# State matmuls of a block attention kernel: two halves of 64 columns in place of one of 128

## The chip, the cores and the metric

The kernel runs on one core of one Trainium2 chip. Its engines are TensorE (matmuls; in the profile PE, and PEld for its weight loads), VectorE (DVE), ScalarE (ACT), GpSimd (POOL) and SyncE (SP), which here issues loads, stores and transposing transfers. The metric is the device time of one execution in microseconds; less is better. A time of the kernel is the median of several executions. A profile is one execution, taken by the hardware's profiler.

## The reference

Two stages follow each other. The first is attention with a decaying state, per batch (4) and head (8), over 768 positions in blocks of 64, with 64 values a head:

```
intra = (qb @ kb.T) * Dmask          # within the block
intra = intra @ vb
inter = (qb * lam_pow) @ kv_state    # what earlier blocks left
out   = intra + inter
kv_state = lam_block * kv_state + (kb * rev_pow).T @ vb
```

The second takes the output as 3072 tokens of 512 values and computes `h = x @ w_in` (2048 wide), `g = h + sin(alpha*h)**2 / alpha`, and `g @ w_out`. Inputs and output are float32; the kernel's matmuls run in bfloat16 and sum in float32.

## The kernel before

The kernel cuts each batch's sequence into six blocks of 128 positions, 24 blocks in all (s = 0 to 23). The decay is multiplied into queries and keys ahead of time (lines 464 and 471), so the state is a plain running sum in a bank of TensorE's accumulation memory, which starts anew with each batch. Two heads share the 128 partitions, so each block has four pairs of heads (`jp`).

What one block needs of TensorE is put into one operation of the planner, `piece_G`, with these parts, issued one after the other by `run`:

- `inter` (line 603): the state times the queries. For each of the four pairs of heads one matmul with the tile `Zd`, 128 by 128, which holds the two heads' 64 by 64 states on its diagonal and zeros elsewhere. The moving operand is 128 columns of `qkT`, taken as two runs of 64.
- `part_S` (line 543) of the next block: keys times queries, eight matmuls, each with 64 rows of the array (64*128).
- `part_O` (line 623): the masked scores `Sm` times the values, eight matmuls, each with 64 columns of the array (128*64); they add to what `inter` left in the same bank.
- `part_Z` (line 568): keys times values, eight matmuls (128*64), added to the state.

`inter` with `Zd` is used from block 13 on, where `wide` is true: for blocks 13 to 17 and 19 to 23 (blocks 12 and 18 begin a batch and have no earlier state). That makes ten groups. In nine of them a `part_S` follows `inter`; the last, of block 23, has none, and `part_O` follows directly. Blocks 1 to 5 and 7 to 11 use another form, line 616: a compact state `Zc` and eight matmuls on 64 rows and 64 columns (64*64).

After the group, VectorE multiplies the scores by the mask (line 552), ScalarE or VectorE copies the block's output into `xT` (line 632), and the state into `Zd` (line 578). The wide layer is done in units: `unit_A` (line 671, four matmuls of 512 columns from `xT`), followed by a sine and a square on ScalarE or GpSimd and a sum on VectorE, and `unit_B` (line 736, four matmuls into the output's bank). `unit_A2` (line 705) is a variant with 256 columns. From block 12 on, units A and B alternate, with one attention group after every three to five pairs of them.

A planner (`_Plan`) sets the order on each engine before the kernel is built: it simulates all operations with durations written by hand and dependences found from the buffers that each reads and writes, and emits one wait for each dependence that the order on one engine does not cover. A group counts there as 0.55 us for `part_O` with `inter` (0.68 in the form with `Zc`), 0.33 for `part_S`, 0.13 for `part_Z` and 0.1 for the whole. A group is one operation: it waits ahead of its first matmul and signals after its last.

Of the kernel before, what the change touches and what calls it, by code (L numbers as in the profile page):

```python
# [32 lines left out]
class _Plan:  # L33
# [20 lines left out]
    def op(self, eng, emit, dur, reads=(), writes=(), dma=None, after=(), issue=0.4, lat=2.6, runs=64):  # L54
        o = _Op(eng, emit, dur, tuple(reads), tuple(writes), dma, after, issue, lat, runs)
        for b in o.reads:
            if b in self.writer:
                o.deps.add(self.writer[b])
        for b in o.writes:
            if b in self.writer:  # L60
                o.deps.add(self.writer[b])
            o.deps.update(self.readers.get(b, ()))
        o.deps.update(after)
        for b in o.reads:
            self.readers.setdefault(b, []).append(o)
        for b in o.writes:
            self.writer[b] = o
            self.readers[b] = []
        o.deps.discard(o)
        o.lead = self.lead  # L70
        self.ops.append(o)
        return o
# [171 lines left out]
def bass_lightning_attn__then__act_snake_kernel(  # L244
# [35 lines left out]
    with es:  # L280

        def sb(name, shape, dt):
            return es.enter_context(nc.sbuf_tensor(name, shape, dt))

        def ring(name, n, shape, dt):
            return [sb(f"{name}_{i}", shape, dt) for i in range(n)]
# [17 lines left out]
        qkT = sb("qkT", [128, RT, 8, 128], BF16)  # L304
        Sm = ring("Sm", 2, [128, 8, 128], BF16)
        Zc = ring("Zc", 2, [128, 4, D], BF16)
        Zd = ring("Zd", 2, [128, 4, 128], BF16)
# [17 lines left out]
        ps = [banks[:, 512 * i:512 * i + 512] for i in range(8)]  # L325
# [4 lines left out]
        def _(_unused_eng):  # L330
# [7 lines left out]
            def bank(i):  # L338
                return ("bank", i)
# [249 lines left out]
            def part_O(s, ob, ob2=None):  # L589
                n, j, jq, u = s % NB, s % R2, s % RT // 2 * 2, slice(64 * (s % 2), 64 * (s % 2) + 64)  # L590
                c, i4 = s // BPC, s % BPC
                obs = [ob, ob] if ob2 is None else [ob, ob2]
                new = (0,) if ob2 is None else (0, 2)
                reads = [("v2", j), ("qT", jq), ("qT", jq + 1), ("Sm", s % 2)]
                wide = n and s > SD
                if wide:
                    reads += [("Zd", (s - 1) % 2, 0), ("Zd", (s - 1) % 2, 1)]
                elif n:
                    reads += [("Zc", (s - 1) % 2)]

                def inter(e):
                    for jp in range(4):
                        ins = e.matmul(  # L603
                            ps[obs[jp // 2]][:, 128 * jp:128 * (jp + 1)].rearrange("p (t x) -> p t x", x=64),
                            Zd[(s - 1) % 2][:, jp, :], qkT[:, jq:jq + 2, jp, u],
                            start=(jp in new), stop=False, skip_group_check=True,
                        )
                    return ins

                def mm(e):  # L610
                    ins = None
                    if n and not wide:
                        for jp in range(4):
                            for h in range(2):
                                r = slice(64 * h, 64 * h + 64)
                                e.matmul(
                                    ps[obs[jp // 2]][r, 128 * jp:128 * (jp + 1)].rearrange("p (t x) -> p t x", x=64),
                                    Zc[(s - 1) % 2][r, jp, :], qkT[r, jq:jq + 2, jp, u],
                                    start=(jp in new), stop=False, skip_group_check=True,
                                )  # L620
                    for jp in range(4):
                        for h in range(2):
                            ins = e.matmul(  # L623
                                ps[obs[jp // 2]][64 * h:64 * h + 64, 128 * jp:128 * (jp + 1)],
                                v2[j][:, 2 * jp + h, :], Sm[s % 2][:, 4 * h + jp, :],
                                start=(n == 0 and jp in new), stop=(jp == 3), skip_group_check=True,
                            )
                    return ins

                def then():  # L630
                  for eng, a0, a1, dur in ((("ACT", 0, 2, 0.45), ("DVE", 2, 4, 0.4)) if ob2 is not None else (((("ACT", 0.73, 0.4), ("DVE", 0.7, 0.0)), 0, 4, 0),)):
                    op(eng, lambda e, a0=a0, a1=a1: (e.copy if e is nc.scalar else e.tensor_copy)(  # L632
                        xT[c % RX][:, a0:a1, BL * i4:BL * (i4 + 1)].rearrange("p a (x t) -> p a t x", t=2),
                        ps[obs[a0 // 2]][:, 128 * a0:128 * a1].rearrange("p (a t x) -> p a t x", t=2, x=64)), dur,
                       [bank(obs[a0 // 2])], [("xT", c % RX, i4, a) for a in range(a0, a1)])

                return mm, (0.55 if wide else 0.68) if n else 0.35, reads, [bank(b) for b in sorted(set(obs))], then, inter if wide else None
# [194 lines left out]
            for i in range(NM):  # L832
                hb = (6, 0, 3, 1, 2, 5)[i % 6] if i < 10 else (3, 0, 1, 2)[i % 4]
                u = unit_A2(0, i // 2 * 2, i % 2, hb) if i < 2 else unit_A(0, i, hb)
# [23 lines left out]
            for i in range(8):  # L858
                unit_A2(1, 2 * i, 1, (5, 6, 4)[(i + 2) % 3])
                for _ in range(2 if i in (0, 4) else 1):  # L860
                    kind, s = pieces.pop(0)
# [68 lines left out]
```

## Time and profile before

| | us |
|---|---|
| median of 3 runs | 223.14 (222.13 to 223.4) |
| profiled execution, its own time | 223.52 |
| its span, first to last instruction | 221.4 |
| TensorE busy | 208.6 |
| ScalarE busy | 155.9 |
| VectorE busy | 122.6 |
| GpSimd busy | 89.1 |

The span is shorter than the execution's own time, which also has what lies around the program's instructions. Line 603 has 40 matmuls in the profile, the first at 98.9 us and the last group at 172.2 us.

A line of a group of instructions or of the timeline names the kernel's line (L603), the operation, the tiles as output<-inputs, the part of the array in use as rows*columns, the shape of the moving operand, and how many instructions there are (x4). Matmuls are pipelined: the end of one is modelled and lies behind the start of the next, so distances are taken from start to start.

### The profile page before, as it was taken

How to read it: one execution, taken by the hardware profiler on the slowest of the kernel's cores; microseconds unless marked ns; L12 is line 12 of the kernel's file. 1: busy time of each engine (PE TensorE's matmuls, PEld its weight loads, DVE VectorE, ACT ScalarE, POOL GpSimd, SP SyncE). 2: the span in 40 equal slices, each digit the busy share in tenths (PEclk: the TensorE clock that was granted, in tenths of full speed). 3: DMA queues.
4: the chain of work that ended last, by engine and by line, in shares of the span. 5: the costliest groups of instructions: out<-in, count | busy, mean ns of one | idle time of the engine just before them, and what ended most of it. 6: DMA issues, size and time to landing. Idle time of an engine off the chain costs nothing.

```text
span 221.4 us, 4062 instructions
## 1 busy us (share of the span) xinstructions
PE 208.6 (94%) x1645; PEld 110.7 (50%) x1645; DVE 122.6 (55%) x184; ACT 155.9 (70%) x277; POOL 89.1 (40%) x100
## 2 busy tenths in 40 slices
PE   3889987899898999999999999999999999999995
PEld 1446433456575785545445444545545444444444
DVE  4687775354777887667655455645465544445100
ACT  3735994347697997788788887877788677778211
POOL 4386763454978776863576103011001011110100
DMA  5999999999999999999999752110110011101112
GB/s 131 236 232 271 206 214 208 217 235 237 233 245 275 242 191 245 219 254 189 276 240 245 155 112 33 47 50 0 47 50 21 26 47 50 47 0 49 75 70 95
DMA packets 83651, 33.31 MB, mean 150 GB/s; under 512 B 63520, under 2 KB 80688, under 8 KB 83632
## 3 DMA queue, kind: packets, MB, share of 16 engines
q1 hardware_dynamic: 76880, 24.25, 53.6%
q0 software_dynamic: 3696, 3.67, 9.9%
q10 hardware_dynamic: 3056, 5.13, 6.4%
q8 instruction: 13, 0.21, 0.4%
q14 instruction: 6, 0.05, 0.1%
HBM read 27.28 MB, written 6.29 MB: 152 GB/s over the span
## 4 chain that ended last, share of the span: by engine, by line
PE 63%; DMA 24%; POOL 4%; SPq 4%; ACT 2%; DVE 1%; issue 1%
PE bank L736 32%; PE bank L671 24%; DMA k<-in_k_dram 10%; DMA q<-in_q_dram 5%; DMA v<-in_v_dram 4%; DMA w<-in_moe_w_in_dram 4%; SPq L342 4%; PE bank L705 3%; PE bank L623 2%; PE bank L543 2%; POOL qk L471 1%; POOL qk L464 1%; PE bank L603 1%; POOL u L720 1%; DVE gT L723 1%
## 5 line engine op out<-in xcount | busy, mean ns | idle before, releaser
L736 PE MATMUL bank<-w,gT 128*128 128x512 bf16 (+1 forms) x400 | 94.8, 371 | 0.0
L688 DVE SCALAR_TENSOR_TENSOR gT<-u,rinv,bank 128x512 bf16<-128x512 bf16 x74 | 54.6, 746 | 51.7 <-ACT u L685 34.2
L671 PE MATMUL bank<-xT,w 128*128 128x512 bf16 x296 | 74.2, 379 | 0.6 <-DVE gT L688 0.6
L681 ACT ACTIVATE t<-bank,alpha 128x512 bf16<-128x512 f32 x74 | 50.6, 686 | 24.1 <-PE bank L671 24.0
L736 PEld LDWEIGHTS bank<-w,gT 128*128 128x128 bf16 x400 | 37.7, 98 | 39.6
L686 POOL TENSOR_TENSOR u<-t 128x512 bf16<-128x512 bf16 x19 | 19.7, 1040 | 80.7 <-ACT t L681 79.7
L671 PEld LDWEIGHTS bank<-xT,w 128*128 128x128 bf16 x296 | 28.5, 98 | 34.9 <-DVE gT L688 1.1
L685 ACT ACTIVATE u<-t 128x512 bf16<-128x512 bf16 x55 | 34.4, 629 | 1.8 <-DVE gT L723 0.3
L552 DVE TENSOR_TENSOR Sm<-bank,mask 128x1024 bf16<-128x1024 f32 x24 | 29.2, 1222 | 10.3 <-PE bank L568 7.7
L464 POOL TENSOR_TENSOR qk<-q,Lq 128x512 bf16<-128x512 f32 x24 | 24.5, 1044 | 21.7 <-DMA q<-in_q_dram 18.1
L471 POOL TENSOR_TENSOR qk<-k,Lk 128x512 bf16<-128x512 f32 x22 | 22.9, 1044 | 7.2 <-DMA k<-in_k_dram 7.0
L749 ACT COPY osb<-bank 128x512 f32<-128x512 f32 (+1 forms) x25 | 14.2, 569 | 14.8 <-PE bank L736 14.8
L705 PE MATMUL bank<-xT,w 128*128 128x256 bf16 x176 | 22.3, 273 | 2.0 <-DVE gT L723 2.0
L723 DVE SCALAR_TENSOR_TENSOR gT<-u,rinv,bank 128x256 bf16<-128x256 bf16 x44 | 19.1, 476 | 7.2 <-POOL u L720 4.1
L715 ACT ACTIVATE t<-bank,alpha 128x256 bf16<-128x256 f32 x44 | 18.5, 471 | 3.3 <-PE bank L705 3.1
L705 PEld LDWEIGHTS bank<-xT,w 128*128 128x128 bf16 x176 | 16.2, 98 | 5.5 <-DVE gT L723 3.0
L473 ACT CAST v<-v 128x512 bf16<-128x512 f32 x18 | 11.0, 615 | 7.6 <-DMA v<-in_v_dram 7.6
L632 ACT CAST xT<-bank 128x512 bf16<-128x512 f32 (+1 forms) x18 | 12.9, 716 | 2.8 <-PE bank L568 1.6
L720 POOL TENSOR_TENSOR u<-t 128x512 bf16<-128x512 bf16 x11 | 11.3, 1039 | 4.7 <-ACT t L715 4.6
L543 PE MATMUL bank<-qkT 64*128 64x128 bf16 x192 | 9.8, 226 | 0.2 <-DVE qkT L493 0.2
L623 PE MATMUL bank<-Sm,v 128*64 128x128 bf16 x192 | 9.9, 225 | 0.0
L829 PE MATMUL bank<-mask,ident 128*128 128x512 bf16 x12 | 5.7, 564 | 3.7 <-DVE mask L429 3.7
(55 smaller groups left out, 111.4 us busy)
## 6 DMA issues: line engine op xcount, KB each, us to landing
k<-in_k_dram SPq DMA_DIRECT2D x24, 256.0 KB, 5.5
v<-in_v_dram SPq DMA_DIRECT2D x24, 256.0 KB, 5.5
q<-in_q_dram SPq DMA_DIRECT2D x10, 512.0 KB, 5.5
out_dram<-osb ACTq DMA_DIRECT2D x19, 256.0 KB, 2.0
w<-in_moe_w_out_dram POOLq DMA_DIRECT2D x4, 512.0 KB, 13.1
w<-in_moe_w_in_dram POOLq DMA_DIRECT2D x3, 512.0 KB, 9.0
q<-in_q_dram SPq DMA_DIRECT2D x4, 256.0 KB, 4.6
ws<-in_moe_w_in_dram SPq DMA_DIRECT2D x2, 512.0 KB, 5.4
```

The lines of the kernel that those rows point to most:

```text
L464: lambda e, a=a: e.tensor_tensor(qk2[:, j:j + 2, 4 * a:4 * a + 4, :], q32[jq][:, 4 * a:4 * a + 4, :, :].rearrange("p h t d -> p t h d"), b ...
L471: lambda e: e.tensor_tensor(qk2[:, j, H:2 * H, :], k32[jl][:, :, :], lk, ALU.mult), 0.7 if s in (0,1) else 1.05,
L552: op("DVE", lambda e: e.tensor_tensor(Sm[s % 2][:, :, :], banks[:, 512 * b0:512 * b0 + 1024].rearrange("p (c i) -> p c i", i=128), mask[:, ...
L671: ins = e.matmul(ps[hb][:, c0:c1], w1[:, kc, 128 * m:128 * (m + 1)], xT[x][:, kc, c0:c1], start=(kc == 0 and c0 == lo), stop=(kc == NKC - ...
L681: op("ACT", lambda e: e.activation(t16[ju][:, w], ps[hb][:, w], ACTF.Sin, scale=alpha[:, m:m + 1]), 0.69 * f, [bank(hb), "alpha"], [("t16" ...
L685: lambda e: (e.activation(u16[ju][:, w], t16[ju][:, w], ACTF.Square) if e is nc.scalar else e.tensor_tensor(u16[ju][:, w], t16[ju][:, w], ...
L686: e.tensor_tensor(u16[ju][:, w], t16[ju][:, w], t16[ju][:, w], ALU.mult)), 0,
L688: op("DVE", lambda e: e.scalar_tensor_tensor(out=gT[g][:, m, w], in0=u16[ju][:, w], scalar=rinv[:, m:m + 1], in1=ps[hb][:, w], op0=ALU.mul ...
L705: ins = e.matmul(ps[hb][:, 256 * i:256 * i + 256], w1[:, kc, 128 * (m + i):128 * (m + i + 1)], xT[x][:, kc, lo:lo + 256], start=(kc == 0 a ...
L715: op("ACT", lambda e, i=i: e.activation(t16[ju][:, 256 * i:256 * i + 256], ps[hb][:, 256 * i:256 * i + 256], ACTF.Sin, scale=alpha[:, m + ...
L723: op("DVE", lambda e, i=i: e.scalar_tensor_tensor(out=gT[g][:, m + i, lo:lo + 256], in0=u16[ju][:, 256 * i:256 * i + 256], scalar=rinv[:, ...
L736: ins = e.matmul(ps[ob][:, w], gT[g][:, m, 128 * s4:128 * (s4 + 1)], w2[:, m, w], start=(m == 0), stop=(m == NM - 1),)
```

## The change

Each of the four matmuls of `inter` becomes two. The first takes the columns 0 to 63 of `Zd`'s tile and writes the output partitions 0 to 63, the second the columns 64 to 127 and the partitions 64 to 127. Both read the same 128 columns of queries on all 128 partitions. What is computed is the same, the zeros of the tile included. The durations that the planner is given are not touched.

```
                 def inter(e):
                     for jp in range(4):
-                        ins = e.matmul(
-                            ps[obs[jp // 2]][:, 128 * jp:128 * (jp + 1)].rearrange("p (t x) -> p t x", x=64),
-                            Zd[(s - 1) % 2][:, jp, :], qkT[:, jq:jq + 2, jp, u],
-                            start=(jp in new), stop=False, skip_group_check=True,
-                        )
+                        for o in (0, 64):
+                            ins = e.matmul(
+                                ps[obs[jp // 2]][o:o + 64, 128 * jp:128 * (jp + 1)].rearrange("p (t x) -> p t x", x=64),
+                                Zd[(s - 1) % 2][:, jp, o:o + 64], qkT[:, jq:jq + 2, jp, u],
+                                start=(jp in new), stop=False, skip_group_check=True,
+                            )
                     return ins
```

## The prediction

> **What bounds the kernel now.** I read three views in this order: the page, for the engine that sets the end; the busy time by stretch, for where that engine has no room; and the order in time on TensorE, for what one group of attention matmuls costs. The page first:
>
> ```profile
> span 221.4 us, 4062 instructions
> ...
> PE 208.6 (94%) x1645; PEld 110.7 (50%) x1645; DVE 122.6 (55%) x184; ACT 155.9 (70%) x277; POOL 89.1 (40%) x100
> ...
> PE 63%; DMA 24%; POOL 4%; SPq 4%; ACT 2%; DVE 1%; issue 1%
> ```
>
> The chain that ended last is mostly TensorE; its DMA share lies early. The busy time by stretch splits the span at 98 us, just before the first matmul that the change touches (98.86 us):
>
> ```profile
> core 0: us, PE busy (x) PEld busy (x) DVE busy (x) ACT busy (x) POOL busy (x), PEclk, DMA share, GB/s
> 0.00:98.00 98.00, 87.86 (x846) 51.19 (x847) 65.02 (x110) 68.49 (x134) 63.55 (x75) 1.00 1.10 227
> 98.00:204.00 106.00, 105.93 (x718) 51.42 (x717) 56.25 (x74) 83.67 (x137) 24.47 (x25) 1.00 0.42 92
> ```
>
> From 98 to 204 us TensorE is busy 105.93 of 106.00 us at a granted clock of 1.00, and the DMA engines are used at 0.42 of their time. Whatever TensorE needs more in there comes out at the end, but for one place shown below. After 204 us there are only matmuls of line 736 and the last stores, none of which is touched.
>
> One group with its neighbours, TensorE in order of time:
>
> ```profile
> 117.16 1.03 PE L671 MATMUL bank<-xT,w 128*128 128x512 bf16 x4
> 118.03 0.39 PE L603 MATMUL bank<-qkT,Zd 128*128 128x128 bf16 x4
> 118.35 0.40 PE L543 MATMUL bank<-qkT 64*128 64x128 bf16 x8
> 118.67 0.41 PE L623 MATMUL bank<-Sm,v 128*64 128x128 bf16 x8
> 118.92 0.29 PE L568 MATMUL bank<-v,qk 128*64 128x64 bf16 x8
> 119.14 1.04 PE L736 MATMUL bank<-w,gT 128*128 128x512 bf16 x4
> ```
>
> The first column is the start, the second the time to the modelled end of the last matmul; since ends overlap the next start, only the distance from start to start is a price. Line 603 is what changes: state (Zd) times queries. The product before the operands is the part of the array in use, rows by columns. The same view of the earlier part has line 616, the state matmuls of blocks 1 to 11, already in eight halves (64*64):
>
> ```profile
> 49.16 1.03 PE L736 MATMUL bank<-w,gT 128*128 128x512 bf16 x4
> 50.12 0.41 PE L616 MATMUL bank<-qkT,Zc 64*64 64x128 bf16 x8
> 50.45 0.41 PE L623 MATMUL bank<-Sm,v 128*64 128x128 bf16 x8
> ```
>
> **The change part by part.** It takes away 40 matmuls and 40 weight loads (four in each of ten groups) and puts in 80 and 80. The planner is given the same 0.55 us for the group as before, so its order of instructions on every engine is unchanged, as are waits, buffers and DMA issues; no queue is passed. The group signals once, on its last matmul, so all that waits for it (the mask multiply of line 552, the copies of lines 632 and 578) can only move by what TensorE loses.
>
> *The matmuls themselves.* Four whole ones take 0.22 us (the chain lists 0.22 for line 603 x4, so 0.056 each). Eight halves with 64 columns are seen in line 623: from its start to that of line 568, which uses the same 128*64 shape, is 118.92 - 118.67 = 0.25 us. That is 0.06 a pair, hence the two halves run beside each other, and a pair costs what one whole matmul cost. The body goes from 0.22 to about 0.23 or 0.24 us.
>
> *Changing the shape.* From line 671 (128*128) to line 603 (128*128) the four matmuls of line 671 take 118.03 - 117.16 = 0.87 us, start to start. From line 736 into line 616 the same four take 50.12 - 49.16 = 0.96. So entering a half-array shape costs 0.09 us, which the group now avoids at its first step and pays between line 603 and line 543 (0.32 for a body of 0.22: 0.10). After the change it is paid at entry, and again towards line 543, where 128*64 becomes 64*128.
>
> That second change of direction, 128*64 to 64*128, is not in the trace. Bounds: nothing, if both count as the same halved array (line 623 to line 568, same shape, adds nothing), and the 0.10 that other changes cost. I take 0.09 to 0.10, since 64*128 to 128*64 (line 543 to 623: 0.32 or 0.33 for eight halves, against 0.25 without a change) costs 0.08 and is its mirror image.
>
> *Sum for one group.* Before: 118.35 - 117.16 = 1.19 us from the start of the last whole unit to the next part. After, by the row of line 616, which has both the entry and an exit to another shape: 50.45 - 49.16 = 1.29, and at 82.52 to 83.82 it is 1.30. I take 1.30: +0.11 us.
>
> The Trainium skill, page "TensorEngine Tiling (Array Packing)", section "Key Properties", says that changing the tiling mode, and not merely the tile, drains TensorE; that speaks against this change, and the trace agrees wherever it has a change of shape (0.08 to 0.10 us). By that rule the unseen change 128*64 to 64*128 is paid like the others, the sum is unchanged, and the chance of the second rival below falls.
>
> *How many groups.* Ten starts of line 603, from 98.86 to 172.19 us. Nine are followed by line 543 as above. The tenth is not:
>
> ```profile
> 171.33 1.03 PE L671 MATMUL bank<-xT,w 128*128 128x512 bf16 x4
> 172.19 0.39 PE L603 MATMUL bank<-qkT,Zd 128*128 128x128 bf16 x4
> 172.51 0.41 PE L623 MATMUL bank<-Sm,v 128*64 128x128 bf16 x8
> ```
>
> There line 603 goes straight to line 623, which has the new shape: the change of shape moves from behind the four matmuls to ahead of them. Cost 0.00, within 0.02.
>
> One of the nine, at 111.47 us, stands ahead of the only visible wait of TensorE in this stretch:
>
> ```profile
> 112.39 0.63 ACT L685 ACTIVATE u<-t 128x512 bf16<-128x512 bf16 x1
> ...
> 112.59 1.04 PE L736 MATMUL bank<-w,gT 128*128 128x512 bf16 x4
> ...
> 112.93 0.71 ACT L632 CAST xT<-bank 128x512 bf16<-128x512 f32 x1
> ...
> 113.70 1.04 PE L671 MATMUL bank<-xT,w 128*128 128x512 bf16 x4
> ```
>
> The unit at 112.59 takes 1.11 us to the next start, where the same unit takes 0.88 at 119.14: TensorE waits 0.23 us for ScalarE's copy into xT. That copy is behind ScalarE's square (112.39 to 113.02); the group's last matmuls, line 568 at 112.37, were done by 112.66. With the group 0.11 later (112.77) the copy still starts at 112.93, and TensorE's loss is covered by its wait. The cover would be gone above 0.23 us. The two groups before it are not covered: the sine at 111.67 that heads this chain was itself released by TensorE (line 671).
>
> Sum: 8 x 0.11 + 0.00 + 0.00 = +0.88 us. The profiled execution took 223.52 us (span 221.4 and 2.1 around it), so it would become 224.4; against the median, 223.14, which is 0.38 lower, 224.0, or +0.4%. The least a measurement of this kernel tells from no change is about 0.5%, 1.1 us (the three runs shown span 222.13 to 223.4), so I expect a small loss just inside that.
>
> **Rivals.**
>
> *1. The halves of a pair do not run beside each other (clearly slower).* The two halves read the same 128 columns of queries on all 128 rows, while in line 623 each half has its own moving tile; or the narrow weight loads become the pace. Then a pair takes twice 0.056, and the body 0.22 more per group. For: no row has two halves with one moving operand. Against: line 623 reads 128 rows for each half, and its pairs cost 0.06; line 568, eight halves with half the columns, is through in 0.22 us including the change back (119.14 - 118.92), so a pair of 64-column weight loads takes under 0.06. Time: eight groups at 0.33 (2.64), the covered one 0.33 - 0.23 = 0.10, the last 0.22, together +2.96: 226.1. It decides early: a group 0.03 us dearer than forecast (pairs of 0.063), nine times, passes 224.26. Half-way, at pairs of 0.09, it is 8 x (0.11 + 0.13) + 0.13 = +2.05: 225.2.
>
> A page rule stands behind this rival: the same tiling page, section "Restrictions", says that column tiling turns off the fast weight load. With the figure of "TensorE: Matmul & The Clock Gate", section "LDWEIGHTS", columns over 1.2 in ns, 64 columns would be an estimated 53 ns and a pair 107 if its loads came one after the other; line 568 does not bear that out.
>
> *2. No change from 128*64 to 64*128 is paid (not slower).* If both shapes count as one halved array, the group is 0.96 + 0.25 = 1.21 us against 1.19: +0.02, eight times, 0.16 us: 223.3. For: the direction is nowhere in the trace. Against: 64*128 to 128*64 does pay (0.08), and so does 64*64 to 128*64 (line 616 to 623: 0.33 to 0.34).
>
> A gain would need a group under 1.19 us. With entry at 0.96 and eight halves at 0.25 even the second rival has none; nothing but the spread of the runs gives one.
>
> **How the numbers follow.** Forecast, 224.0: 0.74; its own spread is 0.6 us either way (half the spread of the three runs), so about four in ten of it lie above 224.26, the bound of half a per cent, counting that the covered group may also show (+0.11). Rival 1, 225.2 to 226.1: 0.11. Rival 2, 223.3: 0.15, of which little falls beyond either bound. So slower 0.74 x 0.42 + 0.11 + 0.02 = 0.44, faster 0.04 from the spread below rival 2, same 0.52. The range goes from 222.9 (rival 2 less two thirds of the spread) to 225.3 (just past the half-way case of rival 1), which leaves out most of rival 1 and the lower tail, under 2 in 10.
>
> **What would show it.** In the changed profile line 603 has 80 matmuls of 128*64. Right: the four matmuls of the unit ahead take 0.96 instead of 0.87, line 603 to line 543 takes 0.33 to 0.34 instead of 0.32, a group is 0.10 to 0.12 longer, the wait ahead of 113.70 shrinks to about 0.12, the tenth group is unchanged, and the span from 98.86 on grows by 0.9 us with other engines' rows as before. Rival 1 would show line 603 to 543 at 0.45 or more; rival 2 at 0.25. Wrong in another way: a new idle of TensorE behind a group, or a shift ahead of 98.86, where nothing is touched.

## The result and the profile after

The changed kernel takes 224.18 us (median of 22 runs, 223.36 to 225.9) against 223.28 us of the kernel before (22 runs beside them, 222.13 to 224.89). The ratio is 1.0041, with a 95% interval of 1.0023 to 1.0059. The loss is therefore real. Its middle, 0.41%, lies below the half per cent that was set as the bound; its interval reaches past it.

The page of the changed kernel's profile, and its busy time in the stretches (columns: length, then busy time and instructions of PE, PEld, DVE, ACT and POOL, granted clock, the DMA packets' summed time as a share of the DMA engines' time, GB/s):

```profile
span 222.5 us, 4142 instructions
...
PE 209.8 (94%) x1685; PEld 109.9 (49%) x1685; DVE 122.4 (55%) x184; ACT 155.9 (70%) x277; POOL 89.1 (40%) x100
```

```profile
0.00:98.00 98.00, 87.86 (x845) 51.04 (x846) 64.86 (x109) 68.10 (x133) 63.46 (x75) 1.00 1.11 227
98.00:204.00 106.00, 106.00 (x754) 50.28 (x753) 56.04 (x73) 83.14 (x137) 24.65 (x25) 1.00 0.43 92
```

TensorE's busy time rises from 208.6 to 209.8 us. The other engines' rows and the stretch ahead of 98 us hardly move (TensorE 87.86 us there in both); the stretch behind it now has no idle TensorE at all by this view, which counts modelled ends and does not show waits as short as those below. The same group as in the prediction, TensorE in order of time (start, length to the modelled end):

```profile
117.56 1.03 PE L672 MATMUL bank<-xT,w 128*128 128x512 bf16 x4
118.51 0.41 PE L604 MATMUL bank<-qkT,Zd 128*64 128x128 bf16 x8
118.86 0.40 PE L543 MATMUL bank<-qkT 64*128 64x128 bf16 x8
119.19 0.41 PE L624 MATMUL bank<-Sm,v 128*64 128x128 bf16 x8
119.43 0.29 PE L568 MATMUL bank<-v,qk 128*64 128x64 bf16 x8
119.66 1.04 PE L737 MATMUL bank<-w,gT 128*128 128x512 bf16 x4
```

(Lines behind 603 have moved down by one.) The unit ahead now takes 0.95 us to the group's first start, where it took 0.87; line 604 to line 543 takes 0.35, where line 603 took 0.32; from the start of the unit ahead to the start of the unit behind it is 2.10 us for 1.98. All behind line 543 is unchanged.

The group of block 15, whose loss should vanish in TensorE's wait for xT (start and length, all engines, other lines left out):

```profile
111.00 1.03 PE L672 MATMUL bank<-xT,w 128*128 128x512 bf16 x4
...
112.78 0.63 ACT L686 ACTIVATE u<-t 128x512 bf16<-128x512 bf16 x1
...
113.10 1.04 PE L737 MATMUL bank<-w,gT 128*128 128x512 bf16 x4
...
113.32 0.72 ACT L633 CAST xT<-bank 128x512 bf16<-128x512 f32 x1
...
114.09 0.39 PE L672 MATMUL bank<-xT,w 128*128 128x512 bf16 x1
```

Its unit ahead in the kernel before:

```profile
110.61 1.03 PE L671 MATMUL bank<-xT,w 128*128 128x512 bf16 x4
```

The next unit starts at 114.09 in the changed kernel. From 111.00 to there is 3.09 us, and it was 3.09 before (110.61 to 113.70): the wait behind the group shrank by what the group grew, from 1.11 to 0.99 us for the unit in it. ScalarE's copy still starts behind its square, not behind the group.

From the start of the last wide matmul ahead of the first changed group to the start of the last matmul of the program, the trace has 119.91 us before and 120.88 after: +0.97 us. The rest of the difference of the two profiled executions (223.52 and 224.64) is 0.14 us ahead of the first group.

### The profile page after: what moved, and what is told of

Read it like the earlier page. It is cut to its first block, busy times and chain, and to the rows that moved or that the text cites. A ratio compares the mean times of both kernels' runs of the same rounds, so it can differ in the third digit from the quotient of the medians.

```text
span 222.5 us, 4142 instructions
## 1 busy us (share of the span) xinstructions
PE 209.8 (94%) x1685; PEld 109.9 (49%) x1685; DVE 122.4 (55%) x184; ACT 155.9 (70%) x277; POOL 89.1 (40%) x100
## 4 chain that ended last, share of the span: by engine, by line
PE 65%; DMA 22%; POOL 4%; SPq 4%; ACT 3%; issue 1%; DVE 0%
PE bank L737 33%; PE bank L672 23%; DMA k<-in_k_dram 10%; DMA q<-in_q_dram 5%; DMA w<-in_moe_w_in_dram 4%; SPq L342 4%; DMA v<-in_v_dram 2%; PE bank L624 2%; PE bank L543 2%; PE bank L706 2%; PE bank L604 2%; ACT t L716 2%; POOL qk L471 1%; POOL qk L464 1%; POOL u L721 1%; ACT u L720 1%
```

## The experiments

The theory: what costs is a change of the part of the array in use, and the group got one more of them; the number of matmuls does not matter. The rival: four more matmuls and four more weight loads a group cost the 0.12 us, 0.03 each. In some traces the record of the first wide matmul behind a group is missing (x3 in place of x4); the distances below are taken where the records are complete.

| kernel | shapes in a group, beginning behind a 128*128 unit | changes | matmuls of the state | one group, ns | first group to last matmul, us | ratio to before (95%) |
|---|---|---|---|---|---|---|
| before | 128*128, 64*128, 128*64, back | 3 | 4 | 1332 | 119.91 | |
| before_again | the same | 3 | 4 | 1332 | 119.91 | 0.9986 (0.996 to 1.0012) |
| changed | 128*64, 64*128, 128*64, back | 4 | 8 | 1454 | 120.88 | 1.0041 (1.0023 to 1.0059) |
| halves_by_O | 64*128, 128*64, back | 3 | 8 | 1332 | 119.91 | 1.0009 (0.9986 to 1.0032) |
| scores_last | 128*64, 64*128, back | 3 | 8 | 1333 | 119.91 | 0.998 (0.995 to 1.0009) |
| whole_by_O | 64*128, 128*128, 128*64, back | 4 | 4 | 1438 | 120.77 | 1.0048 (1.0028 to 1.0068) |
| sixteen | as changed | 4 | 16 | not complete | 121.13 | 1.0077 (1.005 to 1.0104) |
| alternate | 128*128, 128*64, 128*128, 128*64, 64*128, 128*64, back | 6 | 6 | 1681 | 123.06 | 1.0181 (1.0152 to 1.0209) |
| alternate_again | the same | 6 | 6 | 1681 | 123.06 | 1.0131 (1.0086 to 1.0175) |

One group is the time from the start of the last wide matmul ahead of it to the start of the first one behind it, in single records of the trace. The last column but one is the sum over all groups, with the wait that covers one of them. halves_by_O, whole_by_O, alternate and sixteen share one set of runs of the kernel before (median 223.15 us), and before_again, scores_last and alternate_again another (224.21). The same kernel is thus 0.5% apart in the two sets, more than the effect, so each ratio is taken within its own set.

### The halves next to the part that has their shape

```
                     for p in parts:
                         if len(p) > 5 and p[5] is not None:
                             p[5](e)
-                    for p in parts:
                         ins = p[0](e)
```

In `run`, on top of the change. `inter` is now issued just ahead of the values part, behind the scores.

> The eight halves stand between the scores (line 542 here) and the values part, whose 128*64 shape they share. Theory (a change of the array's shape costs about 0.1 us, the number of matmuls nothing): a group has three changes as in the kernel before, so from the unit ahead of a group to the unit behind it nothing is added, 0.00 to 0.01 us a group, and the time is that of before, ratio 1.000 (0.998 to 1.002). Rival (the four more matmuls and weight loads cost 0.12 us a group, 0.03 each): as in the changed kernel, ratio 1.004.

TensorE in order of time, around the second group:

```profile
102.71 1.03 PE L671 MATMUL bank<-xT,w 128*128 128x512 bf16 x4
103.67 0.40 PE L542 MATMUL bank<-qkT 64*128 64x128 bf16 x8
104.00 0.41 PE L603 MATMUL bank<-qkT,Zd 128*64 128x128 bf16 x8
104.24 0.39 PE L623 MATMUL bank<-Sm,v 128*64 128x128 bf16 x8
104.47 0.29 PE L567 MATMUL bank<-v,qk 128*64 128x64 bf16 x8
104.69 1.04 PE L736 MATMUL bank<-w,gT 128*128 128x512 bf16 x3
```

The entry (0.96 us for the unit ahead) is paid for the scores now. Between the halves and line 623 nothing is paid: 0.24 us for eight halves, and line 623 itself goes down from 0.25 to 0.23, since it no longer follows a change. The group is 1332 ns, as before. Eight matmuls in place of four, and no loss: the rival falls.

### The whole matmuls in that place

The same edit on the kernel before.

> The four whole matmuls of the kernel before, moved between the scores and the values part. Theory: the shapes run 128*128, 64*128, 128*128, 128*64, 128*128, four changes in place of three, with not one matmul more; by the seen prices (0.96 into the group, 0.33 across the scores, 0.15 to 0.16 from the last matmul into another shape, 0.02 for the first pair after it) a group is 0.11 us longer, eight of nine groups show it, the last is unchanged: +0.9 us, ratio 1.004. Rival (number of matmuls): nothing, ratio 1.000.

```profile
103.01 1.03 PE L670 MATMUL bank<-xT,w 128*128 128x512 bf16 x4
103.97 0.40 PE L542 MATMUL bank<-qkT 64*128 64x128 bf16 x8
104.30 0.40 PE L602 MATMUL bank<-qkT,Zd 128*128 128x128 bf16 x4
104.62 0.41 PE L622 MATMUL bank<-Sm,v 128*64 128x128 bf16 x8
104.87 0.29 PE L567 MATMUL bank<-v,qk 128*64 128x64 bf16 x8
105.09 1.04 PE L735 MATMUL bank<-w,gT 128*128 128x512 bf16 x4
```

The matmuls of the kernel before, not one more, lose 0.106 us a group and 0.86 us in all once they stand between two other shapes. This and the run before it are the two crossed halves of the test: the loss goes with the number of changes (four), not with the form of the matmuls.

### More changes of shape

```
                     for jp in range(4):
-                        ins = e.matmul(
-                            ps[obs[jp // 2]][:, 128 * jp:128 * (jp + 1)].rearrange("p (t x) -> p t x", x=64),
-                            Zd[(s - 1) % 2][:, jp, :], qkT[:, jq:jq + 2, jp, u],
-                            start=(jp in new), stop=False, skip_group_check=True,
-                        )
+                        for o in (slice(0, 128),) if jp % 2 == 0 else (slice(0, 64), slice(64, 128)):
+                            ins = e.matmul(
+                                ps[obs[jp // 2]][o, 128 * jp:128 * (jp + 1)].rearrange("p (t x) -> p t x", x=64),
+                                Zd[(s - 1) % 2][:, jp, o], qkT[:, jq:jq + 2, jp, u],
+                                start=(jp in new), stop=False, skip_group_check=True,
+                            )
```

> Of the four pairs of heads the first and third go as one whole matmul, the second and fourth as two halves: six matmuls. Theory: whole, halves, whole, halves, scores are four changes of shape where the kernel before has one, three more at 0.096 each, +0.29 us a group; eight groups 2.3, the covered one 0.29 less the 0.23 of its wait, 0.06, the last group two more, 0.17: +2.5 us, ratio 1.011. Rival (number of matmuls): two more a group, half of the changed kernel's loss, +0.5 us, ratio 1.002.

```profile
103.04 1.03 PE L672 MATMUL bank<-xT,w 128*128 128x512 bf16 x4
103.90 0.73 PE L604 MATMUL bank<-qkT,Zd 128*128 128x128 bf16 x6
104.57 0.40 PE L543 MATMUL bank<-qkT 64*128 64x128 bf16 x8
```

(The line of the six shows the shape of the first.) From line 604 to line 543 it is 0.67 us for 0.32: +0.35 with only two more matmuls than before and two fewer than in the changed kernel. The direction is the theory's and far from the rival's 0.06, but the size was missed: three more changes cost 0.349 us, 0.116 each, not 0.096. The single records show why (for a pair of halves, distances are from the start of its second half to the next start). A pair of 128*64 halves that follows a change and is itself followed by one takes 176 ns; the last of four pairs takes 152. Likewise the first of four pairs takes 76 or 77 ns to the second and later ones 52 or 53. So the first pair of 128*64 halves behind a change costs 24 ns more, and these belong to the price of the change. Behind other changes less is added: the first whole matmul takes 65 to 67 ns for 56 (whole_by_O), the first pair of 64*128 takes 62 to 64 for 52 or 53. Here the three gaps give 0.29 us, and the pair, the whole matmul and the pair right behind them 24, 10 and 24 ns more, together 0.35. With 0.35 for each of eight groups, 0.14 for the covered one (0.35 less the 0.21 that its wait still gave), and 0.23 for the last, the sum is 3.16; the trace has 3.15.

The time had risen by 4.0 us (227.16 against 223.15), more than the trace's 3.15, so the kernel was run again, beside an unchanged copy of the kernel before.

> The alternating kernel once more, since its time rose by 4.0 us and TensorE's own row of matmuls from the first group on by 3.15. If the rest lies in the part ahead of 98 us, where nothing was changed, and varies from execution to execution: the trace again shows +3.15 us from the first group on, and the ratio comes nearer to 1.014. If the changes of shape cost something that this trace does not show, the ratio stays at 1.018 and the excess must be behind the first group.

> The kernel before, as it is, for a second profile of it and as a measure of what no change looks like: ratio 1.000 within 0.003; from the last wide matmul ahead of the first group to the last matmul 119.91 us, as in the first profile; the first group's place differs by some tenths of a us.

Both second traces repeat the first ones from the first group on, 123.06 and 119.91 us. What differs is where the first group stands: the last wide matmul ahead of it starts at 98.76 us in the first profile of the alternating kernel and 100.66 in the second, and at 98.64 and 99.18 in the two of the kernel before. The ratio came down to 1.0131, with 1.014 inside its interval. The excess of the first measurement is thus not behind the first group in either trace, and places of the first group that lie 1.9 us apart with the same program are enough for it; that it came from there in those very runs, which have no trace, is not shown.

### More matmuls, no more changes

```
                     for jp in range(4):
-                        for o in (0, 64):
-                            ins = e.matmul(
-                                ps[obs[jp // 2]][o:o + 64, 128 * jp:128 * (jp + 1)].rearrange("p (t x) -> p t x", x=64),
-                                Zd[(s - 1) % 2][:, jp, o:o + 64], qkT[:, jq:jq + 2, jp, u],
-                                start=(jp in new), stop=False, skip_group_check=True,
-                            )
+                        for t in range(2):
+                            for o in (0, 64):
+                                ins = e.matmul(
+                                    ps[obs[jp // 2]][o:o + 64, 128 * jp + 64 * t:128 * jp + 64 * t + 64],
+                                    Zd[(s - 1) % 2][:, jp, o:o + 64], qkT[:, jq + t, jp, u],
+                                    start=(jp in new and t == 0), stop=False, skip_group_check=True,
+                                )
```

On top of the change.

> The changed kernel with each half cut again by its two runs of 64 query columns: sixteen matmuls of 64 columns, all 128*64. Theory: the same changes of shape as the changed kernel; eight pairs of 64 columns take 0.03 each, like line 568, so the body stays at 0.24 to 0.26 and the time is that of the changed kernel, ratio to before 1.004. Rival (number of matmuls): twelve more a group than before, three times the changed kernel's loss, +2.9 us, ratio 1.013.

```profile
117.19 1.03 PE L673 MATMUL bank<-xT,w 128*128 128x512 bf16 x4
118.15 0.44 PE L605 MATMUL bank<-qkT,Zd 128*64 128x64 bf16 x16
118.52 0.40 PE L543 MATMUL bank<-qkT 64*128 64x128 bf16 x8
```

Sixteen matmuls take 0.37 us to the next part, where the eight take 0.35. In single records a pair takes 31 or 32 ns from its first half to the first half of the next, where half of a 128-column pair (56) would be 28. The sum over all groups is 0.25 us above the changed kernel, 0.03 a group for eight more matmuls and eight more weight loads, 3 ns each: a price, but a tenth of the rival's 0.03 us for each. Over the kernel before the rival needs 2.9 us, and the trace has 1.22, most of it the change's own 0.97. The ratio, 1.0077, lies above the theory's 1.004 and its interval holds 1.0055, which the trace gives.

### The scores last

```
-                    for p in parts:
+                    for p in sorted(parts, key=lambda p: len(p) == 5 and p[1] == 0.33):
                         ins = p[0](e)
```

In `run`, on top of the change. The key is true of the scores part alone. The edit holds for the earlier blocks too, which lie ahead of the first group and so outside the trace's distances.

> The changed kernel's eight halves, with the scores part moved to the end of the group: halves, values part and state part (all 128*64) stand together, then the scores (64*128). Theory: three changes of shape a group as in the kernel before, none inside the run of 128*64; entry 309 ns, 25 for the first pair, the parts at their seen lengths, 0.13 from the state part into the scores, 0.15 back: within 0.01 us of the kernel before for a group, ratio 1.000 (0.998 to 1.002). Rival (the halves lose by themselves, and standing next to the values part cured them in the first experiment by another way, for instance by the scores hiding their weight loads): the loss of the changed kernel, 1.004.

```profile
117.99 1.03 PE L672 MATMUL bank<-xT,w 128*128 128x512 bf16 x4
118.94 0.41 PE L604 MATMUL bank<-qkT,Zd 128*64 128x128 bf16 x8
119.19 0.39 PE L624 MATMUL bank<-Sm,v 128*64 128x128 bf16 x8
119.42 0.29 PE L568 MATMUL bank<-v,qk 128*64 128x64 bf16 x8
119.64 0.40 PE L543 MATMUL bank<-qkT 64*128 64x128 bf16 x8
119.97 1.04 PE L737 MATMUL bank<-w,gT 128*128 128x512 bf16 x4
```

The halves stand where the changed kernel has them, first in the group, with the same entry (0.95 us) and the same weight loads; only what follows them has their own shape. 117.99 to 119.97 is 1.98 us, the kernel before to the hundredth. Its ratio, 0.998, is that of an unchanged copy in the same set of runs (0.9986), so it beats neither kernel by anything that these runs tell. No version came out faster than the kernel before.

## Why the prediction was right

- *The bound.* TensorE from 98 us on, with no room: right. The sum of the groups' losses came out at the end but for the one cover that was named.
- *The body.* Four whole matmuls and four pairs of halves cost the same: right. In single records a half starts 3 or 4 ns after its partner, and a pair takes 56 ns from first half to first half, as a whole matmul does. The common moving operand cost nothing, so rival 1 was wrong, and with it the narrow weight loads as the pace: in the sixteen, a pair with its two 64-column loads takes 31 or 32 ns.
- *The entry.* 0.09 us was read from line 616; the records have 309 ns from the last wide matmul into the halves, for 216: 93 ns.
- *The change that the trace of before lacked,* 128*64 to 64*128. It was put at 0.09 to 0.10. It takes 152 ns from the start of the last half, where a pair that no change follows takes 52 or 53, so 0.10. Rival 2 was wrong. The rule of the Trainium skill's page "TensorEngine Tiling (Array Packing)", section "Key Properties", that a change of mode drains TensorE and a change of tile does not, fits each of the shapes tried here. The traces show the price: about 0.1 us wherever rows or columns change, nothing from the halves to line 623 or from there to line 568. That TensorE drains at the change they do not show.
- *The sum for one group.* 0.11 against 0.122 measured. In the records it is 1.183 us before and 1.304 after. Some 0.007 of the shortfall is rounding, since the 1.19 of before is a difference of two rounded starts. The rest is the state matmuls to line 543 in the new kernel, 0.33 to 0.34 foreseen and 0.347 in the records (0.341 for line 616 to the next part), since the way out of 128*64 takes 152 ns and not the 146 of line 616's way out.
- *The groups.* Eight with their full loss, the covered one with none, the last with none (from its unit ahead to the unit behind 171.33 to 172.85 before, 172.44 to 173.97 after; in records the group is 879 ns in both): right. 8 x 0.122 is 0.97, what the trace has; 0.88 was forecast.
- *The time.* 224.0 was forecast and 224.18 measured, +0.4% both. The difference of the two medians, 0.90 us, meets the forecast's 0.88 better than the trace's 0.97 does; with an interval from 0.23 to 0.59%, or 0.5 to 1.3 us, that closeness is luck. So in part is the side of the half per cent on which it fell, which the prediction had put at little better than even.

The price of a change of shape was taken apart less well than it was summed. The prediction's 0.09 to 0.10 did not count the slower first pair as part of the change; it did no harm there, since line 616 as the model of a whole part has it built in (its first pair takes 76 or 77 ns too), and it showed only where changes were added one at a time.

## What to carry to other kernels

Count the changes of the array's shape (rows and columns in use) along TensorE's order, and price each at about 0.11 to 0.12 us where TensorE is the bound (0.106 for the one that whole matmuls added here, 0.122 for the one that halves added); a matmul of 128 moving columns cut into two column halves cost nothing by itself. So put parts with the same shape next to each other, and judge a new shape by its neighbours: the same eight halves cost 0.12 us a group between two other shapes and nothing beside the values part. When no row of the trace has the very form that a change brings, a nearby part with an entry and an exit of the same kind, taken whole, gives a better price than its pieces.

## What was not expected of the hardware

The first pair of 128*64 halves after a change of shape takes 24 ns longer than the next ones (76 or 77 ns for 52 or 53), and the first whole matmul 10 longer, so the three changes that the alternating kernel added cost 0.116 us each rather than the 0.096 that a gap alone shows.

The weight loads (PEld) show how a change looks, though not why it costs what it does. In the kernel before, line 603 keeps the shape of the unit ahead of it (the group of block 15):

```profile
111.26 0.43 PEld L603 LDWEIGHTS bank<-qkT,Zd 128*128 128x128 bf16 x4
111.47 0.39 PE L603 MATMUL bank<-qkT,Zd 128*128 128x128 bf16 x4
```

In the changed kernel line 604 changes it:

```profile
111.95 0.25 PEld L604 LDWEIGHTS bank<-qkT,Zd 128*64 128x64 bf16 x8 [0.42 <-issue]
111.95 0.41 PE L604 MATMUL bank<-qkT,Zd 128*64 128x128 bf16 x8
```

The first load starts 0.21 us ahead of its matmul where the shape stays, and starts together with it where the shape changes. Whether the loads are held back by the matmuls of the old shape, or the new matmuls by their late loads, no run here tells.

One program's first group stood up to 1.9 us apart in two profiled executions (98.76 and 100.66 us), more than the whole effect studied here. The distance from the first group on repeated within 0.01 us, and so one trace told kernels apart whose ratios did so less sharply: the intervals of the changed kernel (1.0023 to 1.0059) and of halves_by_O (0.9986 to 1.0032) overlap.
